# Four v pieces on another queue, and w_in and w_o cut into other 512-byte pieces

## The chip, the core and the metric

The kernel runs on one core of a Trainium2 chip. The core has five engines that run side by side: TensorE (PE in the profile, with its weight loads as PEld), VectorE (DVE), ScalarE (ACT), GpSimd (POOL) and SyncE (SP). They share an on-chip memory of 128 partitions. Inputs are brought from the chip's main memory by 16 DMA engines. A DMA is issued by an instruction on SP, ACT or POOL, and lands later; the semaphore that it raises then releases whoever waits for the data. The metric is the device time of one execution in microseconds (us), as the median of several runs.

## The reference

A polysketch attention over 4 batches, 4 heads, 1088 tokens and head dimension 32, and behind it a feed-forward layer with a squared relu over all 4352 tokens:

```python
def phi(x):                                   # 8 x 8 = 64 features of a token
    a = np.einsum('rd,bhsd->bhsr', S1, x)
    b = np.einsum('rd,bhsd->bhsr', S2, x)
    return np.einsum('bhsi,bhsj->bhsij', a, b).reshape(*x.shape[:-1], r * r)
q_p, k_p = (phi(q), phi(k))
kv = np.einsum('bhsf,bhsd->bhfd', k_p, v)     # not causal: all keys first
z = np.sum(k_p, axis=2)
x = (q_p . kv) / (q_p . z + 1e-06)            # abridged
h = np.maximum(x @ w_in, 0.0)                 # w_in 128 x 2048
out = h * h @ w_out                           # w_out 2048 x 128
```

No token can leave the attention of its batch before all 1088 keys and values of that batch have been read. For the first batch nothing else is there to do in that time.

## The kernel before

**Layout.** A batch's tokens are split over the partitions: token 34·p + g of a head lies on partition row p, so that one row of k, q or v of a head is 4352 contiguous bytes. `vn` holds v with partition 32·p + row, in nine token groups t of 32 numbers for each head. v of the first batch comes in eight DMAs, by `load_v(eng, b, p, t0, t1)`: four pieces p with the token groups 0 to 3 (each a contiguous run of four tokens, 512 bytes for a row and head), and four pieces with the groups 4 to 8 (five tokens, 640 bytes; the last has three). The former hold 64 KB each; of the latter three have 80 KB and one 48 KB.

**Weights.** `load_wi` brings a quarter c of w_in: columns 512·c to 512·c + 511, which is 2048 contiguous bytes in each of 128 rows. `load_wo` brings a quarter of w_out: four blocks of 128 rows, 512 bytes for each partition and block. POOL then casts each quarter of w_in (`cast_wi`, L686). The feed-forward part goes through the 16 blocks d of 128 hidden units in order: `ffn1` (L598) multiplies by `w_in[:, 128 d : 128 d + 128]`, ACT and DVE apply relu and square (L610, L621, L623), and `ffn2` (L642) adds the product with `w_o[:, 128 d : 128 d + 128]` into `po`. The tokens come in ten chunks of 256 to 512; the first has 256 tokens.

**Order of the work.** The start is written out by hand and each engine runs it in that order: PE warm-up matmuls (`keep_warm`, L693); k transposed on DVE (L291); key features on PE (kf, L316), copied by ACT (kb, L322) and multiplied on DVE (kp, L332); the queries' transpose (qT, L297) and their features (x, L755); the sum over the keys (kvp, L397), which reads kp and all of v, the groups 0 to 3 first; then denominators and numerators of the first 256 tokens (L788, L824, L829) up to the first xT (L852). From there a planner (`_Order`) fixes every engine's order with costs that stand in the code. Nothing of the order depends on when a DMA really lands.

**Queues.** SP issues almost all DMAs, in the order of the code: S2, two pieces of k, 256 columns of q, six of the eight v pieces, q's columns 256 to 639, w_in's quarters 0, 1, 2, w_out's 0, 1, w_in's 3, w_out's 2, 3, q's columns 640 to 1087, and then k, v and q of the next batches. POOL issues the other two v pieces (p = 0 and 1, groups 0 to 3), behind the building of `iden` and `sel` and ahead of `sq` (L723), which x needs. SP and ACT together have eight DMA semaphores in turn, so a DMA from SP waits until the one eight places before it has landed; POOL's have their own.

Of the kernel before, what the change touches and what calls it, by code (L numbers as in the profile page):

```python
# [14 lines left out]
def _ap(t: bass.AP, p0: int, np_: int, off: int, free):  # L15
    p = list(t.ap)[0]
    return bass.AP(
        t.tensor, t.offset + p0 * p[0] + off, [[p[0], np_]] + [list(d) for d in free]
    )
# [88 lines left out]
def kernel(  # L108
# [11 lines left out]
    nc = tc.nc  # L120
# [3 lines left out]
    NT = (S + 127) // 128  # L124
# [35 lines left out]
    def sb(name, cols, dt=F32, rows=128):  # L160
        return cpool.tile([rows, cols], dt, tag=name, name=name)
# [9 lines left out]
    w_in32, w_o, w_in = sb("w_in32", 2048), sb("w_o", 2048), sb("w_in", 2048, F32R)  # L171
# [14 lines left out]
    def load_q(eng, b, c0, c1):  # L186
        eng.dma_start(
            qn[b % 2][:, c0:c1],
            bass.AP(q.tensor, q.offset + b * H * S * D + c0, [[G * D, 128], [1, c1 - c0]]),
        )  # L190
# [3 lines left out]
    def first(b, t, p):  # L194
        return NT * p + t if b else 4 * p + t if t < 4 else 16 + 5 * p + t - 4

    def load_v(eng, b, p, t0=0, t1=NT):
        n = 32 * ((t1 if p < 3 else min(t1, NT - 2)) - t0)
        eng.dma_start(
            _ap(vn[b % 2], 32 * p, 32, 32 * t0, [[32 * NT, H], [1, n]]),  # L200
            bass.AP(
                v.tensor, v.offset + b * H * S * D + 32 * first(b, t0, p),
                [[G * D, 32], [S * D, H], [1, n]],
            ),
        )

    def load_wi(eng, c):
        eng.dma_start(
            w_in32[:, 512 * c : 512 * c + 512], moe_w_in[:, 512 * c : 512 * c + 512]
        )  # L210

    def load_wo(eng, c):
        eng.dma_start(
            _ap(w_o, 0, 128, 512 * c, [[128, 4], [1, 128]]),
            bass.AP(
                moe_w_out.tensor, moe_w_out.offset + c * 512 * 128,
                [[128, 128], [128 * 128, 4], [1, 128]],
            ),
        )

# [2 lines left out]
    load_k(nc.sync, 0, 0, 512)  # L223
    load_k(nc.sync, 0, 512, S)
    load_q(nc.sync, 0, 0, 256)
    for t0, t1 in ((0, 4), (4, NT)):
        for p in range(0 if t0 else 2, 4):
            load_v(nc.sync, 0, p, t0, t1)

    zero_a = sb("zero_a", 8)  # L230
    nc.scalar.copy(zero_a[:, :], nc.const_aps.tensor(0.0, (128, 8), F32))
# [26 lines left out]
    nc.gpsimd.tensor_copy(  # L258
        _ap(sel, 0, 16, 64, [[80, 4], [1, 16]]), _ap(iden, 0, 16, 0, [[0, 4], [1, 16]])
    )  # L260
    for p in range(2):
        load_v(nc.gpsimd, 0, p, 0, 4)
    nc.vector.tensor_reduce(
        out=own_h[:, :], in_=_ap(iden, 0, 128, 0, [[32, 4], [1, 32]]), op=add, axis=AX
    )
# [441 lines left out]
    nc.scalar.copy(ss[:, :], sp[:, 0:80])  # L707
    load_q(nc.sync, 0, 256, 640)
    load_wi(nc.sync, 0)
    load_wi(nc.sync, 1)  # L710
    load_wi(nc.sync, 2)
    load_wo(nc.sync, 0)
    load_wo(nc.sync, 1)
    load_wi(nc.sync, 3)
    for c in range(2, 4):
        load_wo(nc.sync, c)
# [453 lines left out]
```

## Time and profile before

| | us |
|---|---|
| median of 3 runs | 184.22 |
| lowest, highest | 184.16, 187.38 |
| the profiled execution: its own time | 184.81 |
| its span, first to last instruction | 183.0 |
| PE busy | 177.6 (97% of the span) |
| ACT, DVE, POOL busy | 136.6, 121.9, 40.1 |
| q1 (SP's DMA queue) | 24128 packets, 10.82 MB |
| q0 (POOL's) | 64 packets, 0.13 MB |

The span leaves 1.8 us of the execution's own time outside it. Below, positions are microseconds from the span's start. A line of the timeline or the chain begins with the start and the duration; `x4` counts instructions; brackets hold the idle time of the engine before it and what ended it. The rows marked SPq or POOLq, and DMA_DIRECT2D on POOL, are issues of DMAs, not the transfers.

### The profile page before, as it was taken

The numbers are of one execution on the slowest core, as the hardware profiler recorded it, in microseconds if no ns is written. First come the engines' busy times: TensorE is split into PE (matmuls) and PEld (weight loads), VectorE is DVE, ScalarE is ACT, GpSimd is POOL, SyncE is SP. The second block draws the span as 40 slices with busy tenths as digits, with TensorE's granted clock in tenths as the row PEclk, the third lists the DMA queues.
The fourth block names the chain that finished last, engine by engine and source line by source line (L and its number), as shares of the span: only waits on it lengthen the run. The fifth ranks groups of instructions, "written<-read, shape, count | busy, mean of one in ns | idle before, by whom it ended". The sixth has DMA issues, their size and how long they took to land.

```text
span 183.0 us, 3998 instructions
## 1 busy us (share of the span) xinstructions
PE 177.6 (97%) x1529; PEld 104.6 (57%) x1529; DVE 121.9 (67%) x262; ACT 136.6 (75%) x259; POOL 40.1 (22%) x160
## 2 busy tenths in 40 slices
PE   8989999999999999999999999999999999999992
PEld 2758876655645655555455554545555555555892
DVE  4988859999999961799994335996353334333640
ACT  3438679849948886799937778894777777777980
POOL 7426408438300002570018100500000000000000
PEclk9999999999999999999999999999999999999999
DMA  4899991010028900000030200003003000300211
GB/s 163 237 289 321 293 234 34 4 32 0 0 36 207 219 0 4 4 2 0 0 54 15 42 0 5 0 0 59 0 4 57 0 0 7 51 0 0 39 22 29
DMA packets 24386, 11.26 MB, mean 62 GB/s; under 512 B 17936, under 2 KB 22800, under 8 KB 24368
## 3 DMA queue, kind: packets, MB, share of 16 engines
q1 hardware_dynamic: 24128, 10.82, 23.7%
q8 instruction: 12, 0.20, 0.5%
q0 software_dynamic: 64, 0.13, 0.3%
q10 hardware_dynamic: 176, 0.07, 0.1%
q14 instruction: 6, 0.05, 0.1%
HBM read 8.78 MB, written 2.23 MB: 60 GB/s over the span
## 4 chain that ended last, share of the span: by engine, by line
PE 97%; DVE 1%; issue 0%; ACT 0%; ACTq 0%
PE po L642 61%; PE pg L598 18%; PE nd L551 3%; PE po L637 2%; PE pol L637 2%; PE warm L693 2%; PE qc L304 2%; PE nd L415 1%; PE kvp L397 1%; PE qc L348 1%; PE kvp L415 1%; PE nd L348 0%; PE x L755 0%; DVE kp L332 0%; PE den L824 0%
## 5 line engine op out<-in xcount | busy, mean ns | idle before, releaser
L642 PE MATMUL po<-g,w_o 128*128 128x512 f32 (+3 forms) x288 | 122.7, 547 | 0.1
L610 ACT ACTIVATE gt<-pg 128x512 f32<-128x512 f32 (+3 forms) x144 | 75.3, 570 | 31.9 <-PE pg L598 31.0
L642 PEld LDWEIGHTS po<-g,w_o 128*128 128x128 f32 x288 | 53.5, 189 | 32.1 <-issue 24.8
L598 PE MATMUL pg<-xT,w_in 128*128 128x512 f32 (+3 forms) x160 | 70.3, 520 | 0.0
L621 ACT ACTIVATE g<-gt 128x512 f32<-128x512 f32 (+2 forms) x102 | 60.7, 623 | 1.6
L623 DVE TENSOR_TENSOR g<-gt 128x512 f32<-128x512 f32 (+3 forms) x43 | 30.0, 699 | 39.8 <-ACT gt L610 39.1
L598 PEld LDWEIGHTS pg<-xT,w_in 128*128 128x128 f32 x160 | 29.2, 190 | 28.3 <-ACT gt L610 11.5
L511 POOL COPY rd<-rc 32x9 f32<-32x9 f32 (+2 forms) x80 | 19.5, 244 | 26.0 <-DVE rc L503 22.8
L457 POOL COPY kv<-kvt 32x64 f32<-32x64 f32 x48 | 12.7, 264 | 44.7 <-DVE kvt L434 42.5
L520 DVE STREAM_SHUFFLE qa<-qc 128x576 f32<-128x576 f32 (+2 forms) x20 | 11.8, 647 | 0.0
L535 DVE TENSOR_TENSOR qp<-qa,qb 128x576 f32<-128x576 f32 (+2 forms) x20 | 10.8, 603 | 0.0
L483 DVE STREAM_TRANSPOSE qt<-qc 128x576 f32<-128x576 f32 (+2 forms) x10 | 5.8, 611 | 6.8 <-PE qc L348 4.7
L368 DVE TENSOR_TENSOR kp<-fs 128x576 f32<-128x576 f32 x12 | 8.7, 742 | 0.0
L646 DVE STREAM_TRANSPOSE oT<-po 128x512 f32<-128x512 f32 (+3 forms) x9 | 5.9, 653 | 2.1 <-PE po L642 2.1
L551 PE MATMUL nd<-qp,kv 32*32 32x288 f32 (+2 forms) x320 | 6.6, 354 | 0.0
L520 DVE STREAM_SHUFFLE qb<-qc 128x576 f32<-128x576 f32 (+2 forms) x10 | 6.1, 648 | 0.0
L568 DVE TENSOR_TENSOR xT<-nd,bc 128x576 fp32r<-128x576 f32 (+2 forms) x10 | 5.6, 593 | 0.5 <-PE nd L551 0.5
L637 PE MATMUL po<-w_o,g 128*128 128x128 f32 x32 | 5.8, 279 | 0.0
L297 DVE STREAM_TRANSPOSE qT<-qn 128x192 f32<-128x192 f32 (+3 forms) x11 | 5.8, 552 | 0.0
L637 PE MATMUL pol<-w_o,g 128*128 128x128 f32 x32 | 5.7, 275 | 0.0
L561 DVE STREAM_TRANSPOSE bc<-rd 128x576 f32<-128x576 f32 (+2 forms) x10 | 5.7, 596 | 0.0
L551 PEld LDWEIGHTS nd<-qp,kv 32*32 32x32 f32 x320 | 2.9, 103 | 3.6 <-issue 2.4
(107 smaller groups left out, 90.8 us busy)
## 6 DMA issues: line engine op xcount, KB each, us to landing
kn<-in_k_dram SPq DMA_DIRECT2D x3, 544.0 KB, 8.6
qn<-in_q_dram SPq DMA_DIRECT2D x3, 544.0 KB, 7.6
vn<-in_v_dram SPq DMA_DIRECT2D x9, 144.0 KB, 7.3
w_in<-in_moe_w_in_dram SPq DMA_DIRECT2D x4, 256.0 KB, 4.5
w_o<-in_moe_w_out_dram SPq DMA_DIRECT2D x4, 256.0 KB, 7.6
out_dram<-oT SPq DMA_DIRECT2D x12, 64.0 KB, 1.9
out_dram<-oT SPq DMA_DIRECT2D x8, 56.0 KB, 3.1
out_dram<-oT SPq DMA_DIRECT2D x8, 48.0 KB, 1.8
```

Of the source, the lines that this page charges most:

```text
L368: nc.vector.tensor_tensor(out=_ap(st[b, "kp"], 0, 128, 64 * NT * h, [[64, NT], [8, 8], [1, 8]]), in0=_ap(fs, 0, 128, o, [[32, NT], [1, 8], ...
L457: nc.gpsimd.tensor_copy(_ap(st[b, "kv"], 32 * c, 32, 64 * h, [[32, E], [1, 32]]), _ap(st["kvt"], 32 * h, 32, 0, [[64, E], [1, 32]]),)
L511: nc.gpsimd.tensor_copy(st[b, "rd", i0][32 * h : 32 * h + 32, n * c : n * c + n], st["rc"][32 * c : 32 * c + 32, n * h : n * h + n],)
L520: nc.vector.stream_shuffle(in_=banks(st[b, "qc", i0], 2 * x, 0, m), out=_ap(st[b, which, i0], 0, 128, 2 * m * x, [[m, 2], [1, m]]), mask=m ...
L535: nc.vector.tensor_tensor(out=st[b, "qp", i0, e][:, r], in0=st[b, f"qa{e}", i0][:, r], in1=st[b, "qb", i0][:, r], op=mult,)
L551: nc.tensor.matmul(nd[32 * h : 32 * h + 32, 512 * c : 512 * c + m], kv[r, o : o + 32], qp[r, m * h : m * h + m], start=(e == 0), stop=(e = ...
L598: nc.tensor.matmul(st["pg", u][:, n * i : n * i + n], w_in[:, 128 * (d0 + i) : 128 * (d0 + i) + 128], xT[:, c0 : c0 + n],)
L610: nc.scalar.activation(gt[:, 0:w], st["pg", u][:, 0:w], Relu)
L621: nc.scalar.activation(to, of, Square)
L623: nc.vector.tensor_tensor(out=to, in0=of, in1=of, op=mult)
L637: nc.tensor.matmul(po[x // 128][:, 0:128], g[:, x : x + 128], w, start=(d == 0), stop=(d == NB - 1),)
L642: nc.tensor.matmul(po[0][:, 0:n], w, g, start=(d == 0), stop=(d == NB - 1))
```

## The change

The loads of v's first batch are shared out otherwise: SP issues the four pieces with token groups 0 to 3, and POOL the four with groups 4 to 8. SP so has two DMAs fewer and POOL two more. A load of w_in no longer takes 512 contiguous columns but four blocks of 128, which lie 512 columns apart; in a row these are four pieces of 512 bytes, 2048 bytes apart. A load of w_out likewise takes four blocks of 128 rows that lie 512 rows apart instead of four that follow each other; it had 512-byte pieces before, and has as many now. In the tiles block j of load c stands at place 4 c + j in both, so the hidden units are gone through in another order, the same for both weights. The bytes are the same in all.

```diff
     def load_wi(eng, c):
         eng.dma_start(
-            w_in32[:, 512 * c : 512 * c + 512], moe_w_in[:, 512 * c : 512 * c + 512]
+            _ap(w_in32, 0, 128, 512 * c, [[128, 4], [1, 128]]),
+            bass.AP(
+                moe_w_in.tensor, moe_w_in.offset + 128 * c,
+                [[2048, 128], [512, 4], [1, 128]],
+            ),
         )
...
-                moe_w_out.tensor, moe_w_out.offset + c * 512 * 128,
-                [[128, 128], [128 * 128, 4], [1, 128]],
+                moe_w_out.tensor, moe_w_out.offset + c * 128 * 128,
+                [[128, 128], [4 * 128 * 128, 4], [1, 128]],
...
-    for t0, t1 in ((0, 4), (4, NT)):
-        for p in range(0 if t0 else 2, 4):
-            load_v(nc.sync, 0, p, t0, t1)
+    for p in range(4):
+        load_v(nc.sync, 0, p, 0, 4)
...
-    for p in range(2):
-        load_v(nc.gpsimd, 0, p, 0, 4)
+    for p in range(4):
+        load_v(nc.gpsimd, 0, p, 4, NT)
```

## The prediction

> **What bounds the kernel.** I read the page's chain first, then the chain in order of time, then the waits and timelines of the first 24 us, where all loads that the change touches land.
>
> ```profile
> PE   8989999999999999999999999999999999999992
> DMA  4899991010028900000030200003003000300211
> ...
> PE 97%; DVE 1%; issue 0%; ACT 0%; ACTq 0%
> ```
>
> PE carries 97% of the chain, and in the trace it has no idle time over 0.03 us behind 14.6 us. So the change can win only what PE idles before, and loses whatever it makes PE wait. The chain of the start:
>
> ```profile
> 5.26 0.22 ACT kb L322
> 5.49 0.02 issue
> 5.51 0.69 DVE kp L332
> 6.20 0.36 DVE qT L297
> 6.56 0.14 issue
> 6.70 0.69 PE x L755 x16
> 7.39 2.25 PE kvp L397 x72
> ...
> 13.31 0.38 issue
> 13.69 0.42 PE qc L304 x18
> 14.10 0.45 PE pg L598 x2
> 14.55 0.04 issue
> 14.59 0.67 PE po L642 x2
> ```
>
> No step of it is a DMA from v or the weights. PE's idle times are 0.45 us before x, 0.34 before L441, 0.38 before the second part of qc, 0.06 before the first po: 1.23 us is all that could be won, 0.7% of 184. The 2% that a measurement of this kernel can tell from no change are 3.7 us.
>
> **Part 1: v on other queues.** The issues now:
>
> ```profile
> 2.31 1.26 POOL L199 DMA_DIRECT2D vn<-in_v_dram  x2
> 2.56 2.83 SPq L199 DMA_DIRECT2D vn<-in_v_dram  x6
> 3.84 0.41 POOL L723 COPY sq<-ss 128x64 f32<-128x64 f32 x2 [0.26 <-ACT ss L707]
> 5.43 0.44 SPq L187 DMA_DIRECT2D qn<-in_q_dram  x1
> 5.91 1.38 SPq L208 DMA_DIRECT2D w_in<-in_moe_w_in_dram  x3
> 9.97 0.61 POOL L686 CAST w_in<-w_in 128x512 fp32r<-128x512 f32 x1 [3.14 <-DMA w_in<-in_moe_w_in_dram]
> 10.93 0.61 POOL L686 CAST w_in<-w_in 128x512 fp32r<-128x512 f32 x1 [0.35 <-DMA w_in<-in_moe_w_in_dram]
> 13.85 0.61 POOL L686 CAST w_in<-w_in 128x512 fp32r<-128x512 f32 x1 [2.30 <-DMA w_in<-in_moe_w_in_dram]
> ```
>
> *SP.* Six v issues take 2.83 us, 0.47 each; two fewer bring every later issue of SP 0.95 us forward: q at 4.5, w_in's first quarter at 4.95.
>
> *POOL.* Two issues take 1.26 us, 0.63 each; four end at 4.83. Behind them wait sq (3.84 to about 4.85 to 5.25), irep, the small memsets and sfk, all some 1.0 us later: POOL's list that ended at 6.83 ends at 7.85. x needs sq at 6.70, L441 needs irep at 11.54, the casts wait for DMAs until 9.97. All hidden; the nearest cover, sq's, is 1.4 us.
>
> *First four token groups of v.* In the trace these pieces landed at 5.80, 6.26, 6.30 and 6.52. kvp's first weight load came at 7.32, held by the second kp, which ended at 7.12. Slack 0.6 us. Now the last of them is SP's fourth v issue, at 3.97 instead of 3.03. Lower end for its landing: the piece that SP issued at 3.99 before landed at 6.92. Upper end: the longest of SP's v rows, 3.7 us, gives 7.67, and with 80 KB more that POOL's queue then carries beside it, at the 227 GB/s of the stretch 6 to 8 us, 0.35 more: 8.0. kvp so starts 0 to 0.9 us late. Nearest is the row of the same place (6.92 + 0.3 = 7.2), at the edge of the 7.12: I take 0.1 us.
>
> *Groups 4 to 8.* Before, they landed at 6.72, 6.92, 7.48 and 7.99; kvp reaches them at about 8.2 (32 of its 72 matmuls at 29 ns each start). POOL's four would be issued by 4.83, the last from 4.2; POOL's rows take 3.3 to 3.5 us from issue to landing: 7.7. The slack grows from 0.2 to 0.5 us. Gain nothing, since PE did not wait.
>
> **Part 2: w_in in small pieces.** The casts start when the quarters land: 9.97, 10.93, 13.85 and 15.86. The third is late because w_out's 512-byte pieces run beside it and, from 10.47, a 16 KB packet of the instruction queue. PE needs the first cast by 11.97 (done 10.58), the third at 15.58 (done 14.46), the fourth at 17.80 (done 16.47): slack 1.1 us or more. The first w_out quarter landed 7.1 us after its issue at 7.34, at 14.46, and the first po ran at 14.59, by PE's order due at 14.53: slack 0.07 us, the tightest in the kernel. Call T the time of one w_in load, 0.96 us by the first two casts. Three lie ahead of that quarter, and all are issued 0.95 earlier, so PE waits only if T passes (0.95 + 0.07)/3 + 0.96 = 1.30 us.
>
> What 512-byte pieces cost is shown by w_out: in 12 to 14 us, where 754 of 877 packets are under 2 KB, the queue moved 311 GB/s at a DMA share of 1.02; in 8 to 10 us, with 233 of 265 packets of 2 KB or more, 242 GB/s at 0.79. By the first row T falls to 0.84 us. The other end is a doubling to 1.92, which no row comes near (the slowest busy stretch, 227 GB/s, gives 1.15). I take 0.84 to 1.15: no effect on PE. Below nothing it can't go: what lands earlier meets a fixed order in which PE was not waiting.
>
> [...]
>
> *w_out* keeps its count of pieces; only the distance between its blocks grows from 64 to 256 KB. No row shows such a distance; it goes into T's bounds.
>
> *SP's queue.* The q issue at 10.65 took 3.35 us instead of the usual 0.43: with 4 x 128 + 4 x 512 = 2560 weight pieces given out it had to wait for room. Now there are 4096, so SP will stall earlier, around w_out's second quarter. Behind it are q's columns 640 on (landed 18.21, read by DVE at 18.74) and the next k (landed 21.04, read at 21.38). These come when the bytes before them have moved; the queue stays full either way. If they were late, DVE has 0.5 and 0.3 us, then its 1.9 us idle before L483 at 24.68, and PE needs kT at 23.85.
>
> **Sum.** +0.1 (kvp) + 0 + 0 = +0.1 us on the profiled 184.81. That execution lies 0.6 over the median; I apply the difference to the median: 184.22 + 0.1 = **184.3**.
>
> **Rivals.**
>
> *A. v is late.* Takes the place of no wait; it is new. It decides where the fourth v issue lands after 7.12. For it: two queues send v at once; against: less lies ahead of it in SP's queue. Half to all of the bound: +0.4 to +0.9, middle 184.9.
>
> *B. The pieces at 2 KB distance are slow* (slower, the other side). T over 1.30 makes PE wait for w_out's first quarter, 3 us for each us of T: at T = 1.92 it is 1.9 us, 186.1. Over 2% it needs T = 2.5, some 105 GB/s. Against: w_out's row; for: each w_in load now touches all 1 MB, which no row shows.
>
> *C. The gap before qc moves.* The 0.38 us at 13.31 has no releaser. A 16 KB instruction packet began at 10.47 (5.5% of 16 engines in 10 to 12 us, so 1.76 us, where the shortest of the twelve took 0.88). If PE waited for those instructions, a faster transfer saves up to 0.38 (183.8 with a prompt v), and a packet half as slow again adds 0.9 (185.1). [...] The trace can't decide.
>
> *D. The change does not act:* pieces merged into 2 KB packets, v as fast as before: 184.2.
>
> **Chances.** Forecast, within 0.3 of 184.3: 0.46. A 0.19. B 0.13, of it 0.10 over 2%. C faster 0.12, slower 0.05. D 0.03. No row shows a way to a gain of 2%: 0.02 for the unseen. So faster 0.02, slower 0.10, within 2% 0.88. The range 183.5 to 186.1 takes in all but B's worst and the unseen.
>
> **What would show it.** SP's w_in issues 0.95 earlier, sq at 4.85, POOL queue 0.29 MB; q1 some 1250 packets more (1536 by w_in, 256 and their semaphore writes fewer by the two v loads); first cast before 9.5; kvp's start at 7.32 to 7.5; first po at 14.6 to 14.7. Wrong if the first po waits for w_o, if x waits for sq, or if PE gaps appear behind 15 us.

## The result, and the profile after

| | before | after |
|---|---|---|
| median of 9 runs, us | 184.55 | 185.33 |
| lowest, us | 184.16 | 185.07 |
| the profiled execution: own time, us | 184.81 | 185.4 |
| its span, us | 183.0 | 183.6 |

The ratio after/before is **1.0053, with a 95% interval from 1.0036 to 1.0071**: about 1.0 us slower by the ratio. One run of before, 187.38 us, was in a slower state and is left out of the ratio, which compares means and not medians. The 1.0 us are far inside the 2%, and yet no accident, since the interval leaves out 1.

The profile's page, after (busy tenths of PE and the DMA engines, DMA queues with packets, megabytes and share, chain by engine):

```profile
PE   8699999999999999999999999999999999999992
DMA  4999991010028900000030200003003000200211
q1 hardware_dynamic: 25376, 10.66, 23.8%
q0 software_dynamic: 176, 0.30, 0.6%
PE 91%; DMA 5%; SPq 1%; POOL 0%; issue 0%; DVE 0%; ACT 0%
```

PE's second slice, 4.6 to 9.2 us, fell from 9 to 6 tenths; the third rose from 8 to 9, and everything behind it reads the same. And DMA, which the chain before doesn't list, now has 5% of it. These are not v's: followed in order of time, the chain of after goes from q's first piece (4.45 us) over the third quarter of w_in (5.05 us) and its cast to ACT's copy `sw` (L841). That cast ended just as the copy began, and the idle time of PE behind `sw` is 0.34 us in all thirteen profiles of the study; so this path of the chain is a coincidence of two times, and the waits tell more. The waits of PE, after (who waited <- for whom: us in total, times, longest):

```profile
PE x L758 <- DVE qT L300: 0.9, 1, 0.9
...
PE kvp L400 <- DMA vn<-in_v_dram: 0.4, 1, 0.4
```

Both lie before 8.3 us. DVE's timeline says what stands behind the first:

```profile
5.38 0.65 DVE L335 TENSOR_TENSOR kp<-kf,kb 128x512 f32<-128x512 f32 x1
6.57 0.45 DVE L300 STREAM_TRANSPOSE qT<-qn 128x256 f32<-128x256 f32 x1 [0.53 <-DMA qn<-in_q_dram]
6.94 2.12 DVE L335 TENSOR_TENSOR kp<-kf,kb 128x512 f32<-128x512 f32 x3
```

The first piece of q had not landed when DVE wanted it, and the second kp stands behind qT on DVE: it ended at 7.59 instead of 7.12. PE's timeline, after:

```profile
7.16 0.69 PE L758 MATMUL x<-qT,sq 32*64 32x256 f32 x16 [0.89 <-DVE qT L300]
8.28 2.32 PE L400 MATMUL kvp<-vn,kp 128*64 128x64 f32 x72 [0.43 <-DMA vn<-in_v_dram]
...
13.88 0.45 PE L307 MATMUL qc<-qT,sw 32*32 32x96 f32 x32
...
15.00 0.67 PE L645 MATMUL po<-g,w_o 128*128 128x256 f32 x2 [0.19 <-PE pg L601]
```

x came 0.46 later than before (6.70), kvp 0.93 later by its first weight load (8.25 against 7.32). At the first po only 0.41 are left, because the 0.38 of idle time before qc, which the profile of before showed, is absent. Whether the change removed it is settled below.

The moved issues, after (POOL's and SP's timelines):

```profile
2.31 2.35 POOL L199 DMA_DIRECT2D vn<-in_v_dram  x4
4.65 0.41 POOL L726 COPY sq<-ss 128x64 f32<-128x64 f32 x2
9.43 0.61 POOL L689 CAST w_in<-w_in 128x512 fp32r<-128x512 f32 x1 [1.78 <-DMA w_in<-in_moe_w_in_dram]
...
2.56 1.85 SPq L199 DMA_DIRECT2D vn<-in_v_dram  x4
4.94 2.16 SPq L208 DMA_DIRECT2D w_in<-in_moe_w_in_dram  x3
```

They begin where the prediction put them: w_in from 4.94, sq at 4.65, the first cast at 9.43. What came out otherwise is when the transfers ended. The stretch from 4.5 to 7 us, first before, then after (stretch, us, busy time of PE, PEld, DVE, ACT, POOL, clock, DMA share, GB/s):

```profile
4.50:7.00 2.50, 2.05 (x78) 1.54 (x80) 2.42 (x6) 0.87 (x4) 2.07 (x12) 1.00 0.88 217
```

```profile
4.50:7.00 2.50, 1.66 (x65) 1.22 (x64) 1.97 (x6) 0.88 (x4) 2.21 (x12) 1.00 0.98 237
```

The 16 DMA engines were at 0.88 already (0.92 in the two later profiles of the kernel before) and are at 0.98 now (1.02 in the second profile of after). A packet's whole time counts in the stretch in which it starts, so a share can pass 1. The rate hardly differs: 217, 240 and 225 GB/s in three profiles of before, 237 and 243 in two of after, while POOL's queue had 288 KB to send in place of 128. The same stretch by queue (packets, MB, share of the 16 engines), first before, then after:

```profile
q1 hardware_dynamic: 788, 0.42, 68.3%
q0 software_dynamic: 63, 0.13, 19.6%
```

```profile
q1 hardware_dynamic: 594, 0.31, 55.9%
q0 software_dynamic: 170, 0.29, 41.7%
```

POOL's queue (q0) sends 0.16 MB more and SP's (q1) 0.11 MB less, and now all four urgent pieces of v go through SP's.

**When a piece lands.** In the trace each load of k, q, v or the weights leaves 16 records on its semaphore, as many as there are DMA engines. I take one for each engine, done with its share; here a landing is the last of the 16. By that, the last of the four urgent pieces of v (groups 0 to 3) landed at 6.52 before and at **8.19** after. (Where an expectation below counts with about 8.0 for it, that is the 15th of the 16, at 8.02.) Two other numbers set the start of kvp, and together they reproduce it in all thirteen profiles of the study to 0.05 us: kvp's first weight load starts 0.18 to 0.21 us after the second kp ends, or 0.05 to 0.10 us after the last urgent piece lands, whichever is later.

| profile | v by POOL | q's first piece | last urgent piece | second kp ends | kvp's first load | first po |
|---|---|---|---|---|---|---|
| before | 128 KB, urgent | 5.72 | 6.52 | 7.12 | 7.32 | 14.59 |
| before, again | 128 KB, urgent | 6.06 | 6.93 | 7.29 | 7.50 | 13.86 |
| before, third | 128 KB, urgent | 5.44 | 6.96 | 7.44 | 7.63 | 14.05 |
| after | 288 KB, later | 6.54 | 8.19 | 7.59 | 8.25 | 15.00 |
| after, again | 288 KB, later | 6.99 | 8.87 | 8.04 | 8.93 | 15.44 |
| e1, v's part alone | 288 KB, later | 6.51 | 8.31 | 7.56 | 8.37 | 14.75 |
| e2, weights' part alone | 128 KB, urgent | 5.82 | 6.59 | 7.21 | 7.40 | 13.92 |
| e3, all v by SP | none | 5.62 | 6.37 | 7.09 | 7.28 | 14.07 |
| b1, e3 and w_in's first by ACT | none | 5.97 | 6.69 | 7.28 | 7.47 | 14.01 |
| e4, POOL's issued from 4.20 | 288 KB, later | 5.34 | 7.37 | 7.06 | 7.42 | 17.97 |
| e5, half by POOL | 128 KB, later | 5.88 | 7.19 | 7.74 | 7.93 | 14.31 |
| e6, four small ones by POOL | 64 KB, later | 5.86 | 7.44 | 6.91 | 7.50 | 13.93 |
| e7, roles swapped | 256 KB, urgent | 7.01 | 8.71 | 8.06 | 8.81 | 15.20 |

Where the fourth column passes the fifth, kvp goes by v; elsewhere it goes by kp.

### The profile page after: what moved, and what is told of

The parts are those of the page before. It is cut to its first block, busy times and chain, and to the rows that moved or that the text cites. A ratio compares the mean times of both kernels' runs of the same rounds, so it can differ in the third digit from the quotient of the medians.

```text
span 183.6 us, 4001 instructions
## 1 busy us (share of the span) xinstructions
PE 177.2 (97%) x1529; PEld 104.4 (57%) x1529; DVE 121.9 (66%) x262; ACT 136.5 (74%) x259; POOL 41.4 (23%) x162
## 4 chain that ended last, share of the span: by engine, by line
PE 91%; DMA 5%; SPq 1%; POOL 0%; issue 0%; DVE 0%; ACT 0%
PE po L645 61%; PE pg L601 18%; PE nd L554 3%; DMA w_in<-in_moe_w_in_dram 3%; DMA qn<-in_q_dram 2%; PE po L640 2%; PE pol L640 2%; PE qc L307 2%; PE nd L418 1%; PE qc L351 1%; PE kvp L418 1%; SPq L181 0%; PE nd L351 0%; POOL w_in L689 0%; PE x L444 0%
```

## The experiments

Every one of them computes all of the reference. Theory T1: the DMA engines are full between 4.5 and 7 us (a share of 0.88 before, 0.98 after), so pieces that POOL's queue sends at that time push back the urgent ones, wherever SP issues these. Its rivals look for the cause in the weights' part (theory 2), in the place that SP's queue gives to the fourth piece (theory 3), in the mere number of POOL's loads (theory 5), or in a precedence of POOL's packets (theory 6, T6). Some expectations also carry my first reading, that the gap of 0.38 before qc belongs to the kernel before and the weights' part takes it away.

**e1, v's part alone.** Against the changed kernel, the weights' loads are those of before:

```diff
-            _ap(w_in32, 0, 128, 512 * c, [[128, 4], [1, 128]]),
...
+            w_in32[:, 512 * c : 512 * c + 512], moe_w_in[:, 512 * c : 512 * c + 512]
...
-                moe_w_out.tensor, moe_w_out.offset + c * 128 * 128,
+                moe_w_out.tensor, moe_w_out.offset + c * 512 * 128,
```

> v's new split alone, the weights loaded as before. Theory 1 (sharing: POOL's pieces, wanted later, run beside SP's urgent ones and make these and q late): the first kvp weight load at 8.2 to 8.4 us instead of 7.32; the gap of 0.38 us before qc is not touched by this part and stays; 0.7 to 1.0% slower than before. Theory 2 (the weights' pieces cost the time): kvp at 7.3 to 7.4, same time as before within 0.2%. Theory 3 (issue order: SP's fourth v issue simply comes 0.94 us later): as theory 1 here.

Measured 185.22 us against 184.38: 1.0064 (1.0039 to 1.0089), a little under the 0.7 to 1.0% of theory 1. The chain in order of time, e1:

```profile
3.98 4.33 DMA vn<-in_v_dram
8.40 2.32 PE kvp L396 x72
```

SP's fourth v load, issued at 3.98, is 4.33 us under way and stands in the chain right ahead of kvp. All of the loss is there with v's part alone. A gap before qc was expected to stay and is not there.

**e2, the weights' part alone.** v's loops are those of before:

```diff
-    for p in range(4):
-        load_v(nc.sync, 0, p, 0, 4)
+    for t0, t1 in ((0, 4), (4, NT)):
+        for p in range(0 if t0 else 2, 4):
+            load_v(nc.sync, 0, p, t0, t1)
...
-    for p in range(4):
-        load_v(nc.gpsimd, 0, p, 4, NT)
+    for p in range(2):
+        load_v(nc.gpsimd, 0, p, 0, 4)
```

> w_in and w_o in the new pieces alone, v as before. Theory 1: kvp at 7.3, the gap before qc gone or nearly so, since the instruction packet then meets a queue in which no engine lags: 0.1 to 0.3% faster than before. Theory 2: 0.4 to 0.6% slower. Theory 3: as theory 1.

Measured 184.45 against 184.38: 1.0011 (0.9997 to 1.0024). No loss and no gain to be seen; the expected gain of 0.1 to 0.3% isn't there either, and neither is a gap before qc.

**The kernel before, profiled again**, to see whether that gap is a property of it:

> The kernel before, profiled once more. If PE's 0.38 us gap ahead of the second part of qc belongs to the kernel, it is there again at about 13.3 us; if it comes from where an instruction packet falls in this one execution, it has another size or is gone, and the span is then 0.3 to 0.4 us shorter.

It took 184.23 us. PE's timeline, the kernel before in its second profile:

```profile
13.10 0.45 PE L304 MATMUL qc<-qT,sw 32*32 32x96 f32 x32
...
13.86 0.64 PE L642 MATMUL po<-g,w_o 128*128 128x256 f32 x2
```

The 32 matmuls of qc run in one go (no bracket), and the first po starts at 13.86, 0.73 earlier than in the profile that the prediction had. The third profile:

> The kernel before, a third profile: kvp at 7.3 to 7.6 as in both others. The gap of 0.38 us before qc was there once and not in the second execution; if it is gone again, the first po comes at 13.8 to 14.0 and the first profile was an unlucky one there.

184.41 us, no gap before qc, first po at 14.05. No profile of the study but the first has the gap. So it was a chance of one execution, whose cause stays open, and the change did not remove it. Set against the two later profiles, the first po of after (15.00, 15.44) is 0.95 to 1.6 us late, which agrees better with the ratio's 0.7 to 1.3 us than the 0.41 against the first profile.

**After, profiled again:**

> The changed kernel, profiled once more. Theory 1: again q's first piece at 6.3 to 6.7, the fourth urgent v piece at 7.8 to 8.2, the first kvp weight load at 8.1 to 8.5, and no gap over 0.1 us before the second part of qc.

185.84 us. The mechanism is the same, and larger: q's first piece 6.99 (0.3 above the expected range), last urgent piece 8.87 (7.8 to 8.2), kvp from 8.93 (8.1 to 8.5), no gap before qc. PE's waits of this run are easily misread:

```profile
PE kvp L400 <- DVE kp L335: 0.7, 1, 0.7
```

The view names kp, not v. The third kp ended at 8.90, but in the first profile of after kvp started at 8.25 while the third kp ended at 8.45, so kvp doesn't wait for that one; the second had ended at 8.04. The last record of the fourth piece, 8.87, fits by the 0.06 us seen in the other runs. The view had only named what ended last.

**e3, all of v by SP, the urgent pieces first.** The weights' part stays:

```diff
-    for p in range(4):
-        load_v(nc.sync, 0, p, 0, 4)
+    for t0, t1 in ((0, 4), (4, NT)):
+        for p in range(4):
+            load_v(nc.sync, 0, p, t0, t1)
...
-    for p in range(4):
-        load_v(nc.gpsimd, 0, p, 4, NT)
```

> All eight v pieces by SP, the first four token groups ahead, nothing by POOL; the weights in the new pieces. SP's four urgent issues come at the same times as in the changed kernel (2.56 to 4.0 us). Theory 1: q's first piece lands on all engines by 5.2, the fourth urgent piece by 7.0, the first kvp weight load by 7.4; 0 to 0.3% faster than before. Theory 3: the fourth urgent piece lands at 7.8 to 8.0 all the same, kvp at 8.1 to 8.3, 0.4 to 0.6% slower. Theory 2: 0.4 to 0.6% slower with kvp at 7.3.

Measured 184.2 against 184.38: 0.9999 (0.9983 to 1.0015). SP issues the fourth urgent piece at 3.99 here as in the changed kernel, and it landed at 6.37, not at 8.19. So its place in SP's queue is not the cause, and the rival that goes by it falls. PE's timeline and the stretch of the loads, e3:

```profile
7.28 2.32 PE L399 MATMUL kvp<-vn,kp 128*64 128x64 f32 x72
```

```profile
4.50:7.00 2.50, 2.12 (x81) 1.50 (x80) 2.50 (x6) 0.88 (x4) 2.08 (x12) 1.00 0.80 194
```

The engines moved less than in the changed kernel, 194 against 237 GB/s, and the urgent pieces came 1.8 us earlier: what moved was what was wanted next. It gains nothing on the kernel before, since there v was early enough; kvp waits for kp in both. q's first piece came at 5.62, on 15 engines at 4.94; by 5.2 was expected.

**e4, POOL's four v loads moved down, behind the two copies to sq**, issued from 4.20 on:

```diff
-    for p in range(4):
-        load_v(nc.gpsimd, 0, p, 4, NT)
...
+    for p in range(4):
+        load_v(nc.gpsimd, 0, p, 4, NT)
```

> The changed kernel with POOL's four loads moved behind sq, so that their pieces start some 2 us later. Theory 1: q's first piece by 5.2, SP's four by 7.0, the first kvp weight load by 7.4 us; then PE waits inside kvp for POOL's last piece, which lands at 9.3 to 9.8: 0.5 to 0.9% slower than before. Theory 3: SP's fourth still lands at 7.8 to 8.0 and kvp starts at 8.1 or later.

Measured 187.6 against 184.38: 1.0155 (1.0114 to 1.0196), about twice the expected loss. The first half of the expectation came true: x at 6.63, kvp from 7.42. Then PE's timeline and the stretch behind it, e4:

```profile
7.46 1.15 PE L398 MATMUL kvp<-vn,kp 128*64 128x64 f32 x32
11.07 2.11 PE L398 MATMUL kvp<-vn,kp 128*64 128x64 f32 x40 [2.47 <-DMA vn<-in_v_dram]
```

```profile
8.00:11.00 3.00, 0.61 (x21) 0.47 (x17) 1.22 (x2) 0.58 (x1) 1.80 (x11) 1.00 0.98 285
11.50:14.80 3.30, 3.30 (x47) 2.85 (x45) 0.83 (x5) 0.27 (x1) 0.64 (x2) 0.50 1.10 322
```

POOL's pieces now compete with w_in, which SP issues from 4.93; the last one landed at 10.94, and kvp stood in its middle for 2.47 us. And after a stretch in which PE was busy for 0.61 of 3.0 us, the granted clock was 0.50 until 14.88. These two make the first po 17.97. The low clock is the smaller part of the loss, and not every execution has it: two of the four kept a mean granted clock of 1.0 and took 186.52 and 186.71, 1.2% over before, while the profiled one, at 0.988, took 188.5. The dilemma of POOL's later pieces shows: early they push the urgent ones back (8.19 in after), late they are pushed back themselves (10.94 here).

**e5, half of it:** two later pieces (128 KB) by POOL, two by SP, weights as before:

```diff
     for p in range(4):
         load_v(nc.sync, 0, p, 0, 4)
+    for p in range(2):
+        load_v(nc.sync, 0, p, 4, NT)
...
-    for p in range(4):
+    for p in range(2, 4):
         load_v(nc.gpsimd, 0, p, 4, NT)
```

> Weights as before. SP issues the four urgent v pieces and then two of the later ones; POOL issues only the other two of the later ones (80 and 48 KB, as many bytes as before on POOL's queue). SP's fourth urgent issue is at 3.98 us as in the changed kernel. Theory 1 (POOL's bytes run beside SP's urgent ones and take their place): with the bytes of before on POOL the fourth piece lands by 7.2, first kvp weight load at 7.3 to 7.5; 0 to 0.2% slower than before. Theory 3 (issue order): fourth piece at 7.8 to 8.0, 0.5% slower.

Measured 184.51 against 184.41: 0.9994 (0.9973 to 1.0015). The last urgent piece landed at 7.19 (15 engines at 6.92), between e3 and after. kvp's 7.93 in this profile isn't v's doing: k's second piece landed at 5.38 on one engine (the 15 others at 4.73), kf stopped 0.34 us for it, and the second kp ended at 7.74.

**e6, four small loads by POOL**, one token group each (16 KB), so that the count of POOL's loads stays and the bytes fall to 64 KB:

```diff
+    for p in range(4):
+        load_v(nc.sync, 0, p, 5, NT)
...
-        load_v(nc.gpsimd, 0, p, 4, NT)
+        load_v(nc.gpsimd, 0, p, 4, 5)
```

> Weights as before. POOL issues four loads as in the changed kernel, but of one token group each (128-byte pieces, 16 KB a load, 64 KB in all instead of 288); SP issues the four urgent pieces and behind them the groups 5 to 8. Theory 1 (bytes beside the urgent ones): the fourth urgent piece lands by 6.9, kvp starts by 7.4. Rival theory 5 (four loads from POOL disturb the DMA engines whatever their bytes, or POOL's later sq is what counts): fourth piece at 7.6 or later, or x held by sq, kvp at 7.8 or later. The time is 0 to 0.4% over before by theory 1, since SP's weight issues come 0.95 later and the first w_out quarter with them.

Measured 184.62 against 184.41: 1.0003 (0.9982 to 1.0023). The last urgent piece landed at 7.44, between the two expectations (by 6.9, and 7.6 or later): 64 KB in pieces of 128 bytes seem to weigh more than 128 KB in pieces of 640 (e5: 7.19). That is a hint that bytes are not all of it, and no more, since each has one profile and those of one kernel differ by 0.4 to 0.7 us. PE's kvp waited 0.35 for v here, and as the second kp was early (6.91), kvp still began at 7.50. This profile, the longest of e6's runs (185.3), also shows a wait further on: q's columns 640 on landed at 20.13 (15 engines at 18.14), DVE stood 1.15 us for them, and PE 0.80 us until 22.52 for an xT that DVE makes behind. The prediction had looked at this cover ("If they were late"); in this one execution it was too small.

**e7, the roles swapped:** POOL the four urgent pieces, SP the four later ones, weights as before:

```diff
-        load_v(nc.sync, 0, p, 0, 4)
+        load_v(nc.sync, 0, p, 4, NT)
...
-        load_v(nc.gpsimd, 0, p, 4, NT)
+        load_v(nc.gpsimd, 0, p, 0, 4)
```

> The roles exchanged, weights as before: POOL issues the four urgent v pieces, SP the four later ones, at the same issue times as in the changed kernel. If the DMA engines simply share between the two queues (theory 1), the urgent ones are as late on POOL as on SP: the fourth lands at 7.7 to 8.4, kvp starts at 8.0 to 8.6, 0.4 to 0.8% slower than before. If POOL's larger packets get ahead of SP's small ones (theory 6), the fourth urgent piece lands by 7.3 and the time is that of before within 0.2%.

Measured 186.09 against 184.47: 1.0107 (1.0043 to 1.0171). PE's timeline, e7:

```profile
8.84 2.32 PE L396 MATMUL kvp<-vn,kp 128*64 128x64 f32 x72 [0.52 <-DMA vn<-in_v_dram]
```

The urgent pieces by POOL landed at 6.11, 6.86, 8.27 and 8.71, SP's later ones beside them at 7.32 to 8.49. If POOL's packets had precedence, this would have been the good arrangement; T6 falls. It lost more than T1's 0.4 to 0.8%, at least by the middle of its interval; one of its four executions (187.79, mean granted clock 0.991) makes the difference, and the other three alone average 0.7%.

**b1, e3 with w_in's first quarter issued by ACT.** In e3 that quarter landed late (11.60) and PE stood 0.31 us at 12.31 for its cast.

```diff
-    load_wi(nc.sync, 0)
...
+    load_wi(nc.scalar, 0)
```

> All eight v pieces by SP and the weights in the new pieces, as in the run with all v by SyncE, but w_in's first quarter is issued by ACT behind its kb copies (about 6.5 us) instead of by SP at 6.84. If the 0.31 us that PE waited there at 12.31 for the first cast is what kept that version at the time of before, the quarter lands by 11.0, the gap goes, and the time is 0.15 to 0.3% under before. If one DMA engine lags because of an instruction packet whatever the issue time, the quarter lands at 11.3 or later and the time stays within 0.15% of before.

Measured 184.63 against 184.41: 0.9998 (0.9977 to 1.0019). The quarter landed at 11.50 (15 engines at 10.76), as the second expectation has it (11.3 or later, the time within 0.15%); the first is not borne out. The gap at 12.3 is gone all the same, because kvp began 0.19 later than in e3, and the time is no better; a gain of this size can't be told from none here. No kernel of the study beats the one before.

## Why the prediction was right and where it was wrong

The time, 185.33, lies in the range 183.5 to 186.1, and within 2% was the likeliest class. But the case named likeliest, no effect to within 0.3 us, did not come. Rival A did, at the upper end of its size: kvp 0.93 us late of "+0.4 to +0.9", and 1.0 us on the clock. That its size fits is partly luck. Its 0.9 counted a landing at 8.0 from the end of the second kp; by the rule of the table kvp would then start at 8.06, 0.74 late. The 0.93 came from a landing beyond that bound.

**The step that failed** is the landing of the fourth urgent piece. The bound was 6.92 to 8.0, and I took the end near 7.2 because it came from "the row of the same place" in SP's queue. It landed at 8.19, 8.87 and 8.31 in the three profiles with this split. Two things were wrong in it.

The row came from another company. In the kernel before, the load issued at 3.99 shared the engines with 128 KB from POOL, and those were urgent pieces themselves. In the changed kernel 288 KB run beside it. As an estimate, 288 KB at the 237 GB/s of the stretch are 1.24 us; e3 and b1, with nothing from POOL, had 6.37 and 6.69, so 7.6 to 7.9 comes out, nearer to 8.19 than anything that I worked out. I had counted 80 of the 288 KB, as 0.35 us at the upper end, and named no row for the 0.3 us of the end that I took. e3, e5 and after (none, 128 and 288 KB: 6.37, 7.19, 8.19) are the dose, with one or two profiles each; e6 hints that it isn't bytes alone.

And the view that warned of this was in hand and not used: the DMA share of that stretch was 0.88 already, in the kernel before. The two profiles of after show what the larger second queue did there: the share is 0.98 and 1.02, the rate 237 and 243 GB/s against 217 to 240, and the urgent pieces landed 1.2 to 1.9 us later (8.19 and 8.87 against 6.96, the latest of before).

**A term that was missing:** q's first piece. It is issued at 2.09, ahead of all v, and was taken as given; in the cover of x I looked at sq alone. In the profiles with 256 KB or more by POOL from 2.3 on it landed at 6.51 to 7.01, in all others at 5.34 to 6.06. By way of qT that moves the second kp to 7.56 to 8.06. In after, with v in time, kvp would so have begun at about 7.8 (7.59 + 0.19) instead of 7.32, 0.47 late. But v's landing alone, with q in time, gives the whole 0.93; q's lateness lies hidden behind it. Late too, because of q, was SP's third w_in load: by the eight semaphores in turn it has to wait for q's first piece, and it was issued at 6.56, right behind 6.54. Why a load that is issued first is overtaken, the runs show only in part: in after 15 of the 16 engines had done their share of it by 4.92, and one took until 6.54.

**Right:** the start of SP's weight issues (4.94; 4.95 was worked out), sq, q1's 1248 packets more (1250), q0's 0.30 MB, the first cast before 9.5; sq's cover; that the weights' part does nothing to PE (e2). The quarters of w_in landed at 9.37, 10.20 and 11.61, so T is 1.12 on average (0.84 to 1.15 was taken), and w_out's first quarter came at 12.55, 2.4 us ahead of the first po, and nobody waits there. Rival B fell with that; its T of 1.92 no run shows. The slack of 0.07 us, "the tightest in the kernel", was one execution's: in the other two profiles of before w_out's first quarter landed at 13.37 and 12.89, 0.5 and 1.2 us ahead of the first po. In the first, 15 engines were done by 12.82 and one took until 14.46; likewise w_in's third quarter (12.07 and 13.80), which the prediction put down to w_out's pieces as well.

**Not as said, but without a cost:** "all are issued 0.95 earlier" held for the first weight load alone. The issue of a w_in load in the new pieces took 0.62 to 0.69 us (the first three in e2 and in e3) where the kernel before took 0.33 to 0.43, and the third waited for q. So w_out's first issue came at 7.14, 0.2 us earlier. That SP "had to wait for room" at 10.65 was my reading of that one row; in after, with the 4096 pieces, no issue of SP in the first 24 us took over 1.47 us. That SP's queue fills earlier isn't shown either: w_out's last two issues took 2.46 us from 9.41 and q's next 0.65 from 11.91 in place of 3.35 from 10.65, but the kernel before, in its second profile, also stalled from 9.14. No PE wait followed in either profile of after.

**Groups 4 to 8** landed at 8.45, not by 7.7: POOL's loads took 3.8 to 4.4 us from issue to landing instead of 3.3 to 3.5. kvp reached them at 9.23, so the later start of kvp covered it.

**Rival C** rested on a gap that was one execution's chance. It was priced from one profile; three profiles of before show it once. Its 0.38 us were also part of the "1.23 us that could be won", and without them the first profile has 0.85 us; the second has 0.34, the third 1.19, of it 0.59 because k's second piece was late. That PE waited in that gap for the instruction packet of 10.47 (1.76 us) no run shows: in after a packet of the same 16 KB ran from 9.98 for 0.88 us, and no gap followed before qc.

## What to carry to other kernels

Here 288 KB on a second queue hardly raised what the DMA engines moved (217 to 240 GB/s before, 237 and 243 after): at a share of 0.88 to 0.92 already, the pieces that were wanted later and went out by another queue took their time from those that were wanted first (8.19 and 8.87 against 6.52 to 6.96). One queue in the order of need (e3) brought the urgent pieces 1.8 us earlier, at 194 GB/s. When a load's landing is estimated from another load's row, count all that both queues send beside it, and follow each first consumer (here q's as well as v's) to the engine behind which the next step stands.

## What the runs showed of the hardware

- In e4 a wait of 2.47 us inside kvp, in a stretch of 3 us (8 to 11) with PE busy for 0.61, was followed by half the granted clock for 3.4 us (11.47 to 14.88). In the 3.41 us before it fell, PE was busy for 0.94. Two of e4's four executions kept a mean granted clock of 1.0. In all thirteen profiles the recorded stretches at full clock last a multiple of 3.41 us (6.83 and 170.67 in e4, 177.49 or 180.91 elsewhere).
- In some loads one of the 16 engines was far behind the rest: q's first piece 4.92 on 15 engines and 6.54 on the last (after), the fourth urgent piece 6.26 and 7.37 (e4), w_in's first quarter 9.45 and 11.49 (e2), there with a 16 KB packet of the instruction queue of 1.76 us from 8.25 on. What reads such a load came behind the last engine: in e4 kvp's first weight load at 7.42, in e2 the cast at 11.54. What holds the engine in the first two cases stays open; no 16 KB packet of the instruction queue runs there (after 2 us the first begin at 9.98 and 10.18).
- w_in in pieces of 512 bytes showed no cost: from 8 to 10 us the DMA engines moved 322 GB/s (after) and 256 (e2) with them, 242, 226 and 299 with rows of 2 KB (before, three profiles). The spread within one kernel, 226 to 299, would hide a small effect.
